# A linear attention fused with a routed MLP: the seam changed in three places, and the order inside one attention unit

## Chip, cores and metric

The kernel runs on one core of a Trainium2 chip. The metric is the device time of one execution in microseconds (us); smaller is better.

## What is computed

Two computations follow each other. The first is a linear attention with a decaying state (batch 4, 8 heads, 768 steps, head size 48); the second is a mixture of experts with 8 experts (3072 rows of 384, hidden size 1024), where each row goes through one expert, chosen by its logits, and is scaled by its gate. Cut to what matters:

```
for t in range(S):
    cur = einsum('bhd,bhe->bhde', u * k[t], v[t])
    y[t] = einsum('bhd,bhde->bhe', r[t], state + cur)
    state = w[t][..., None] * state + einsum('bhd,bhe->bhde', k[t], v[t])
x = y as rows of 384
logits = x @ w_gate + modality_bias[modality_id]
e_idx = argmax(logits, axis=1)
probs = exp(logits - max); probs /= probs.sum() + 1e-09
for e in range(E):
    mask = e_idx == e
    out[mask] = gate_w[mask] * (relu(x[mask] @ w1[e]) @ w2[e])
```

All data are float32.

## The kernel before

**Attention.** The 3072 rows are cut into 24 units of 128 steps. The loop `for i in range(-2, NU)` (NU = 24) calls `att_iter(i)`, which works on three units at once: it prepares unit a = i + 2, forms the products of unit m = i + 1 and finishes unit z = i. Preparing means two scans on VectorE (`B` backwards, L316, and `E` forwards, L322, with a reciprocal between them), then `K` (`mk_k`, L252) and `G = r * k` (L330) on GpSimd, and `R` (`mk_r`, L249) on VectorE, whose input ScalarE has copied to PSUM (`r_psum`). TensorE turns `K` (`turn`, L285), multiplies `K` with `R` (L371), uses `G` for the diagonal term (`delta`), updates the state `pU_st` and forms the output in `pY` (L410, L413). ScalarE scales the state and copies it to `SPb` (L260, L263). GpSimd computes `dV` (L326), and the row `xp` is `pY` plus `dV` (`x_rows`, L450 on VectorE, or L448 on GpSimd in some units).

**Routing.** `logits` (L467) multiplies finished rows with the gate's weights into the PSUM tile `pR_x`, which also holds the work areas of the routing and of the table below. The routing runs twice: for the first ten units and for the other fourteen (`CUT = (0, 10, 24)`). `route_a` finds the winning expert with five VectorE instructions (L500 to L506), `route_x` the gate's denominator: an exponential on ScalarE (L515), then three sums (L517) and an addition (L518) on GpSimd. `route_b` ranks the rows in each expert and gives each its place, `posT`. From then on `drain(1)` at the end of each unit sends one unit's finished rows to DRAM with an indirect DMA from GpSimd (`scatter`, L666), sorted by expert, into `xs`. Parts of the routing are hung into `att_iter` by a list `hooks`, from which each unit takes one entry.

**MoE.** It works on blocks of 512 rows (q = 0 to 5, the last with 416) and a half block. The expert of block 0 is known early, from the bias. Block 0's rows are loaded from `xs` by four DMAs, one per 128 rows (`rows_load`, L690, issued in unit i = NU - 3 behind the scatters). `blk_t(0)` transposes them on TensorE into three PSUM banks `pX`, `pK`, `pY` (L714: row block j = 0 to 3, in each of them three chunks of 128 features), and splits them into a rounded part `xh` (ScalarE, L722) and the rest `xo` (VectorE, L717), since float32 is computed with three fast products. `blk_up(q, f)` then computes piece f = 0 to 7 of the hidden layer: nine matmuls (L736), a relu on ScalarE (L745) and the rest of the split `h` on VectorE (L747). Two PSUM accumulators take turns in block 0. `w_split` splits the weights (L234, L235 and L240, L241).

**The table.** Which expert and which rows block 1 takes is computed by `table(0)`, a generator of small VectorE instructions on `pR_x` that is advanced with `next(tb)`. `loads()` finishes it, and then SyncE issues the loads of block 1, which read the table. `s` counts the pieces; `logits(NU - 1)`, the gate's logits of the last unit, are issued at s = 2.

**What sets the order.** Each engine carries out its instructions in the order in which this program issues them. A scheduler doesn't move them; a framework places the waits between engines.

## Time and profile before

| | |
|---|---|
| median of three runs | 337.26 us (335.92 to 337.66) |
| profiled execution, its own time | 336.07 us |
| its span, first to last instruction | 334.2 us |
| busy share of the span | TensorE 96%, VectorE 64%, ScalarE 61%, GpSimd 59% |
| mean granted clock of TensorE | 0.998 of full speed |

The profile is of one execution. Its span leaves out 1.9 us around the first and the last instruction. A share of busy time is a mean over the attention (up to about 118 us), the seam between it and the MoE, and the MoE, and the engines are used differently in each. In a row of the timeline the first number is the start, the second the time, then come engine, line of the kernel, operation, output and inputs; what stands in brackets at the end is how long the engine stood idle before it, and who released it. PE is TensorE, DVE is VectorE, ACT is ScalarE, POOL is GpSimd, SP is SyncE.

### The profile page before, as it was taken

The numbers are of one execution on the slowest core, as the hardware profiler recorded it, in microseconds if no ns is written. First come the engines' busy times: TensorE is split into PE (matmuls) and PEld (weight loads), VectorE is DVE, ScalarE is ACT, GpSimd is POOL, SyncE is SP. The second block draws the span as 40 slices with busy tenths as digits, with TensorE's granted clock in tenths as the row PEclk, the third lists the DMA queues.
The fourth block names the chain that finished last, engine by engine and source line by source line (L and its number), as shares of the span: only waits on it lengthen the run. The fifth ranks groups of instructions, "written<-read, shape, count | busy, mean of one in ns | idle before, by whom it ended". The sixth has DMA issues, their size and how long they took to land. (4 is left out here: it accounts for less than half of the span.)

```text
span 334.2 us, 10519 instructions
## 1 busy us (share of the span) xinstructions
PE 320.0 (96%) x4086; PEld 292.3 (87%) x4086; DVE 213.8 (64%) x381; ACT 202.4 (61%) x451; POOL 197.7 (59%) x227
## 2 busy tenths in 40 slices
PE   7889999899989999999999999999999999999993
PEld 3689899898989977899889988998899889999992
DVE  6999999899998646795435945925550564054230
ACT  3877877698679956642423667765755855732150
POOL 7998899789999785676461870256034604440041
PEclk9999999999999999999999999999999999999999
DMA  7966778868778632426346055027444863360010
GB/s 263 370 210 198 240 224 268 265 188 249 226 236 283 206 91 97 95 101 228 124 151 182 0 151 183 0 73 174 179 167 165 234 218 94 95 214 2 2 75 29
DMA packets 32755, 54.73 MB, mean 164 GB/s; under 512 B 17665, under 2 KB 22457, under 8 KB 32696
## 3 DMA queue, kind: packets, MB, share of 16 engines
q1 hardware_dynamic: 29592, 44.51, 43.4%
q0 software_dynamic: 3104, 9.47, 7.5%
q8 instruction: 34, 0.56, 0.7%
q14 instruction: 25, 0.20, 0.2%
HBM read 53.92 MB, written 12.67 MB: 199 GB/s over the span
## 5 line engine op out<-in xcount | busy, mean ns | idle before, releaser
L235 POOL TENSOR_TENSOR wl<-raw,wh 128x768 fp32r<-128x768 f32 x20 | 38.5, 1929 | 73.7 <-ACT wh L234 73.6
L234 ACT CAST wh<-raw 128x768 fp32r<-128x768 f32 x48 | 39.4, 830 | 39.2 <-PE pU_d L758 24.6
L747 DVE SCALAR_TENSOR_TENSOR h<-pS_u,h 128x512 fp32r<-128x512 f32 (+2 forms) x39 | 23.2, 608 | 38.1 <-ACT h L745 31.8
L778 POOL DMA_INDIRECT out<-ot,xg x24 | 25.7, 1069 | 29.4 <-ACT ot L787 23.5
L235 DVE TENSOR_TENSOR wl<-raw,wh 128x768 fp32r<-128x768 f32 x28 | 31.0, 1113 | 15.1 <-ACT wh L234 14.8
L736 PE MATMUL pS_u<-xh,wh 128*128 128x512 f32 (+1 forms) x102 | 39.6, 389 | 0.0
L736 PE MATMUL pS_u<-xo,wh 128*128 128x512 f32 (+1 forms) x102 | 39.3, 385 | 0.0
L736 PE MATMUL pS_u<-xh,wl 128*128 128x512 f32 (+1 forms) x102 | 39.2, 384 | 0.0
L745 ACT ACTIVATE h<-pS_u 128x512 fp32r<-128x512 f32 (+1 forms) x34 | 19.8, 586 | 27.1 <-PE pS_u L736 25.3
L758 PE MATMUL pX_d<-wh,h 128*128 128x384 f32 x96 | 32.3, 337 | 0.0
L758 PE MATMUL pY_d<-wh,h 128*128 128x384 f32 x96 | 32.2, 335 | 0.0
L758 PE MATMUL pK_d<-wh,h 128*128 128x384 f32 x96 | 32.1, 334 | 0.0
L666 POOL DMA_INDIRECT xs<-xp,posT x24 | 26.2, 1092 | 9.2 <-issue 7.1
L330 POOL TENSOR_TENSOR G<-in 128x512 f32<-128x512 f32 x24 | 30.6, 1276 | 0.0
L316 DVE TENSOR_TENSOR_SCAN B<-in,pX_d 128x516 f32<-128x516 f32 x24 | 29.3, 1221 | 1.8 <-DMA in<-rkw 1.8
L252 POOL TENSOR_TENSOR K<-in,B 128x512 f32<-128x512 f32 x24 | 28.4, 1184 | 2.5 <-DMA in<-rkw 1.2
L322 DVE TENSOR_TENSOR_SCAN E<-in,pX_d 128x516 f32<-128x516 f32 x24 | 29.4, 1223 | 0.4
L758 PE MATMUL pU_d<-wh,h 128*128 128x384 f32 x80 | 26.7, 334 | 0.0
L747 DVE SCALAR_TENSOR_TENSOR h<-pT_u,h 128x512 fp32r<-128x512 f32 (+2 forms) x17 | 9.6, 577 | 24.6 <-ACT h L745 24.5
L413 PE MATMUL pY<-v,A 128*64 128x48 f32 x368 | 25.1, 222 | 0.0
L413 PEld LDWEIGHTS pY<-v,A 128*64 128x64 f32 x368 | 23.7, 138 | 0.0
L371 PE MATMUL pS<-R,K 64*64 64x128 f32 (+1 forms) x768 | 22.1, 250 | 0.5 <-DVE R L249 0.4
(246 smaller groups left out, 890.7 us busy)
## 6 DMA issues: line engine op xcount, KB each, us to landing
raw<-w SPq DMA_DIRECT2D x24, 768.0 KB
in<-rkw SPq DMA_DIRECT2D x60, 192.6 KB
v<-vt SPq DMA_DIRECT2D x24, 288.0 KB
xl<-xs SPq DMA_DIRECT2D x24, 192.0 KB
wg<-wf SPq DMA_DIRECT2D x8, 576.0 KB
raw<-w SPq DMA_DIRECT2D x16, 192.0 KB
xs<-zt SPq DMA_DIRECT2D x12, 193.0 KB
in<-rkw SPq DMA_DIRECT2D x3, 512.0 KB
```

The costliest lines, as they stand in the source:

```text
L234: nc.scalar.copy(out=wh[k][:, sl], in_=raw[k][:, sl])
L235: (eng or (nc.vector, nc.gpsimd)[k]).tensor_tensor(out=wl[k][:, sl], in0=raw[k][:, sl], in1=wh[k][:, sl].bitcast(F32), op=ALU.subtract)
L252: nc.gpsimd.tensor_tensor(out=wt(a, "K", [P, 4, P]), in0=quarters(k), in1=quarters(T["B", a][:, 1:517])[:, :, 1:129], op=ALU.mult)
L316: nc.vector.tensor_tensor_scan(out=Bt[:, 516:0:-1], data0=w[:, 516:0:-1], data1=d1[:, 516:0:-1], initial=0.0, op0=ALU.mult, op1=ALU.max)
L322: mark["E", i] = nc.vector.tensor_tensor_scan(out=Et, data0=w[:, 0:516], data1=d1[:, 1:2].to_broadcast([P, 516]), initial=1.0, op0=ALU.mul ...
L330: mark["G", i] = nc.gpsimd.tensor_tensor(out=wt(a, "G", [P, 512]), in0=r, in1=k, op=ALU.mult)
L413: nc.tensor.matmul(out=yh[64:P, g, sw, hh], lhsT=A[:, hh, g, 1 + sw], rhs=vs[:, g, hh] if sw else v[:, h * D:(h + 1) * D], start=new and n ...
L666: rows_apart("xs", nc.gpsimd.indirect_dma_start(out=xs[:, :], out_offset=bass.IndirectOffsetOnAxis(ap=posT[:, n:n + 1], axis=0), in_=T["xp ...
L736: nc.tensor.matmul(out=pp, lhsT=wsrc[0][:, f, c * P:(c + 1) * P], rhs=xsrc[:, c], start=(n == 0), stop=(n == 3 * KC - 1))
L747: nc.vector.scalar_tensor_tensor(out=h2[:, o:o + c1 - c0], in0=pp[:, c0:c1], scalar=0.0, in1=hh[:, c0:c1].bitcast(F32), op0=ALU.max, op1=A ...
L758: nc.tensor.matmul(out=X["y", q][j], lhsT=hsrc[:, j * P:(j + 1) * P], rhs=wsrc[1][:, f], start=(f == 0 and n == 0), stop=(last and n == 2))
L778: ins = nc.gpsimd.indirect_dma_start(out=out[:, :], out_offset=bass.IndirectOffsetOnAxis(ap=xg[0:n, j, 1:2].bitcast(I32), axis=0), in_=ot[ ...
```

## The change

It has five edits.

1. In unit i = 12 (`CUT[1] + 2`, the thirteenth), `route_a(0)` is no longer called from `hooks` at the end of unit i = 11, but behind the unit's backward scan and its reciprocal.
2. `route_x(0)` moves from the start of unit i = 12 to its end, directly ahead of the first `drain(1)`.
3. The last `G` (i = NU - 3) is computed by VectorE behind `R`, and no longer by GpSimd.
4. `blk_t(0)` splits block 0's rows in two groups of columns, 384 and then 128 (`slice(0, 3 * P)` and `slice(3 * P, BT)`), in each of them first the three `xh`, then the three `xo`. The other blocks are as before.
5. `table(0)` yields at two more places. Its twelve instructions behind the first sums are spread over s = 0 and s = 1, and `loads()` moves from s = 0 to s = 2.

```diff
+    def mk_g(i, eng, r, k):
+        mark["G", i] = eng.tensor_tensor(out=wt(i + 2, "G", [P, 512]), in0=r, in1=k, op=ALU.mult)
...
             nc.vector.reciprocal(out=w[:, 0:516:129], in_=Bt[:, 1:517:129])
+        if i == CUT[1] + 2:
+            list(route_a(0))
...
             mk_k(a, k)
-            mark["G", i] = nc.gpsimd.tensor_tensor(out=wt(a, "G", [P, 512]), in0=r, in1=k, op=ALU.mult)
+            if i < NU - 3:
+                mk_g(i, nc.gpsimd, r, k)
...
             mark["R", i] = mk_r(a)
+            if i == NU - 3:
+                mk_g(i, nc.vector, r, k)
...
             vec.tensor_reduce(out=te, in_=cm, axis=AX.X, op=ALU.add)
+            if ph == 0:
+                yield
...
                 tt(out=cm, in0=bc(i8), in1=t[:, :, None].to_broadcast(sh), op=ALU.is_equal)
+                if ph == 0:
+                    yield
...
-        def rest(m):
-            nc.vector.tensor_tensor(out=xo[m], in0=xt[m], in1=xh[m].bitcast(F32), op=ALU.subtract)
-
-        for m in range(KC):
-            if q:
-                rows_turn(q, m, w // 32, xt[m])
-            nc.scalar.copy(out=xh[m], in_=xt[m])
+        def high(m, c=slice(0, w)):
+            nc.scalar.copy(out=xh[m][:, c], in_=xt[m][:, c])
+
+        def rest(m, c=slice(0, w)):
+            nc.vector.tensor_tensor(out=xo[m][:, c], in0=xt[m][:, c], in1=xh[m][:, c].bitcast(F32), op=ALU.subtract)
+
+        for c in (slice(0, 3 * P), slice(3 * P, BT)) if q == 0 else ():
+            for m in range(KC):
+                high(m, c)
+            for m in range(KC):
+                rest(m, c)
...
         if i == CUT[1] + 1:
-            ra, tb = route_a(0), table(0)
-            hooks.extend([lambda: list(ra), lambda: hook_b(0)])
-        if i == CUT[1] + 2:
-            route_x(0)
+            tb = table(0)
+            hooks.extend([lambda: None, lambda: hook_b(0)])
         if i >= NU - 2:
-            hooks.append(lambda: next(tb))
+            hooks.append(lambda i=i: next(tb) if i == NU - 2 else None)
...
+        if i == CUT[1] + 2:
+            route_x(0)
         drain(1)
...
             blk_up(q, f)
-            if s == 0:
+            if s < 2:
+                next(tb), next(tb)
+            if s == 2:
                 loads()
             if s == 2:
                 logits(NU - 1)
```

What this moves, engine by engine, is read from the two built programs. First GpSimd in unit i = 12, before (`ex` holds the exponentials, `xp` the rows with the gate's denominator as one more column):

```order
L510 COPY xp_392<-tidi 128x10
L517 TENSOR_TENSOR ex_1594<-ex_1594 128x10x4
L517 TENSOR_TENSOR ex_1594<-ex_1594 128x10x2
L517 TENSOR_TENSOR ex_1594<-ex_1594 128x10
L518 TENSOR_SCALAR xp_392<-ex_1594 128x10
L326 TENSOR_TENSOR dV_1606<-v_1373,dT_1537 128x384
L252 TENSOR_TENSOR K_1608<-in_91,B_1600 128x512
L330 TENSOR_TENSOR G_1610<-in_91 128x512
L666 DMA xs<-xp_392,posT 29184x386
```

and now:

```order
L518 COPY xp_392<-tidi 128x10
L331 TENSOR_TENSOR dV_1600<-v_1373,dT_1537 128x384
L252 TENSOR_TENSOR K_1602<-in_91,B_1586 128x512
L255 TENSOR_TENSOR G_1604<-in_91 128x512
L525 TENSOR_TENSOR ex_1712<-ex_1712 128x10x4
L525 TENSOR_TENSOR ex_1712<-ex_1712 128x10x2
L525 TENSOR_TENSOR ex_1712<-ex_1712 128x10
L526 TENSOR_SCALAR xp_392<-ex_1712 128x10
L678 DMA xs<-xp_392,posT 29184x386
```

The three sums and the addition have moved behind `dV`, `K` and `G`; they stand directly ahead of the first scatter, which waits for the addition.

Second, ScalarE at the seam, where it rounds block 0's rows, with the engine that each instruction waits for in brackets. Before:

```order
L461 COPY xT_2884<-pT_('x', 0)_2883 128x384 [waits PE_49]
L722 CAST xh_2890<-pX_x_0_2894 128x512 [waits PE_49]
L722 CAST xh_2890<-pK_x_1_2895 128x512 [waits PE_49]
L722 CAST xh_2890<-pY_x_2_2896 128x512 [waits PE_49]
L461 COPY xT_2917<-pT_('x', 1)_2916 128x384 [waits PE_49,Activation_49]
```

and now:

```order
L469 COPY xT_2884<-pT_('x', 0)_2883 128x384 [waits PE_49]
L729 CAST xh_2890<-pX_x_0_2894 128x384 [waits PE_49]
L729 CAST xh_2890<-pK_x_1_2895 128x384 [waits PE_49]
L729 CAST xh_2890<-pY_x_2_2896 128x384 [waits PE_49]
L729 CAST xh_2890<-pX_x_0_2894 128x128 [waits DVE_49]
L729 CAST xh_2890<-pK_x_1_2895 128x128 [waits DVE_49]
L729 CAST xh_2890<-pY_x_2_2896 128x128 [waits DVE_49]
L469 COPY xT_2923<-pT_('x', 1)_2922 128x384 [waits PE_49,Activation_49]
```

Three casts have become six. The first three wait for TensorE as the wide ones did (for its transposes of the fourth row block), the last three for VectorE's subtraction of 384 columns from the same bank.

Third, VectorE in the first pieces of block 0: the end of the table, with `h` of the pieces 0 and 1. Before:

```order
L575 TENSOR_TENSOR pR_x<-cs,pR_x 128x8
L576 TENSOR_TENSOR pR_x<-pR_x,hd_2832 128x8
L577 TENSOR_REDUCE t2(0, 1)_2930<-pR_x 128x1
L579 TENSOR_TENSOR t2(0, 1)_2930<-pR_x,t2(0, 1)_2930 128x1
L747 SCALAR_TENSOR_TENSOR h_0_2977<-pS_u_0_2967,h_0_2977 128x512
L582 SCALAR_TENSOR_TENSOR pR_x<-pR_x,t2(0, 1)_2930 128x1
L583 TENSOR_SCALAR tab<-pR_x 128x1
L585 TENSOR_SCALAR tabe<-pR_x 128x1
L586 TENSOR_SCALAR tab<-pR_x 128x1
L589 SCALAR_TENSOR_TENSOR tab<-pR_x,e0f 128x1
L606 TENSOR_TENSOR fA<-fA,hd_2832 128x8
L747 SCALAR_TENSOR_TENSOR h_1_3035<-pS_u_1_3025,h_1_3035 128x512
```

and now, where `h` of piece 0 follows the reciprocal that ends the split of the rows:

```order
L746 RECIPROCAL xg_2727<-xg_2727 128x4
L767 SCALAR_TENSOR_TENSOR h_0_2970<-pS_u_0_2960,h_0_2970 128x512
L615 TENSOR_SCALAR fs_2828<-pR_x 128x9
L616 SCALAR_TENSOR_TENSOR fA<-pR_x,fs_2828 128x8
L574 TENSOR_TENSOR pR_x<-pR_x,cs 128x8
L575 TENSOR_REDUCE pR_x<-pR_x 128x1
L579 TENSOR_TENSOR pR_x<-pR_x,fA 128x8
L580 TENSOR_REDUCE pR_x<-pR_x 128x1
L581 TENSOR_TENSOR pR_x<-cs,pR_x 128x1
L584 TENSOR_SCALAR pR_x<-pR_x 128x1
L585 TENSOR_TENSOR pR_x<-cs,pR_x 128x8
L767 SCALAR_TENSOR_TENSOR h_1_2995<-pS_u_1_2985,h_1_2995 128x512
```

The `h` of piece 0 now goes ahead of the table's twelve instructions, and the `h` of piece 1 ahead of the last three of them and of the five that end with the writing of `tab` (below the rows shown). The order on TensorE and SyncE is unchanged.

## Rows read from the trace of the kernel before

**Rows 1.** Busy time by stretch: us, PE, PEld, DVE, ACT, POOL busy (x instructions), clock, DMA share, GB/s

```profile
140.00:160.00 20.00, 20.00 (x112) 19.39 (x111) 13.78 (x41) 7.85 (x13) 13.53 (x19) 1.00 0.42 150
```

**Rows 2.** Timeline of POOL, the first two scatters and the last one

```profile
66.11 0.87 POOL L517 TENSOR_TENSOR ex<-ex 128x40 f32<-128x40 f32 x3 [1.93 <-ACT ex L515]
67.06 0.28 POOL L518 TENSOR_SCALAR xp<-ex 128x10 f32<-128x10 f32 x1
...
71.50 1.19 POOL L666 DMA_INDIRECT xs<-xp,posT  x1 [0.86 <-POOL G L330]
...
73.50 1.19 POOL L252 TENSOR_TENSOR K<-in,B 128x512 f32<-128x512 f32 x1
...
76.08 1.02 POOL L666 DMA_INDIRECT xs<-xp,posT  x1 [0.17 <-issue]
...
109.94 1.27 POOL L330 TENSOR_TENSOR G<-in 128x512 f32<-128x512 f32 x1
111.38 1.01 POOL L666 DMA_INDIRECT xs<-xp,posT  x1 [0.17 <-issue]
```

**Rows 3.** Waits of SP's queue: us in total, times, longest

```profile
SPq L690 <- DMA xs<-xp,posT: 2.4, 1, 2.4
```

**Rows 4.** Timeline of PE at the seam

```profile
119.53 0.38 PE L714 MATMUL pX_x<-cs,xl 128*128 128x128 f32 x1 [0.17 <-DMA xl<-xs]
...
120.00 0.38 PE L714 MATMUL pX_x<-cs,xl 128*128 128x128 f32 x1
...
121.08 0.38 PE L714 MATMUL pX_x<-cs,xl 128*128 128x128 f32 x1 [0.46 <-DMA xl<-xs]
...
122.86 0.50 PE L736 MATMUL pS_u<-xo,wh 128*128 128x512 f32 x1
```

**Rows 5.** Timeline of DVE, unit 13's routing and the end of the attention

```profile
64.33 0.24 DVE L500 TENSOR_REDUCE mx<-pR_x 128x10 f32<-128x80 f32 x1 [1.07 <-PE pR_x L467]
...
112.94 0.56 DVE L450 TENSOR_TENSOR xp<-pY,dV 128x384 f32<-128x384 f32 x1 [1.30 <-PE pK L285]
```

**Rows 6.** Timeline of ACT in unit 13

```profile
65.79 0.24 ACT L515 ACTIVATE ex<-pR_x 128x80 f32<-128x80 f32 x1 [0.64 <-DVE oh L506]
...
70.22 0.64 ACT L263 COPY SPb<-pU_st 64x192 f32<-64x192 f32 x2
```

**Rows 7.** Line of the scatter: POOL's queue events, ns min/median/max, first and last start

```profile
L666 POOLq EVENT_SEMAPHORE  x1: 2474/2474/2474, 68.1 to 68.1; - x1
```

**Rows 8.** Timeline of PE, the transposes of unit 15's K

```profile
75.16 0.27 PE L285 MATMUL pT<-cs,K 64*128 64x64 f32 x1
```

**Rows 9.** Timeline of DVE at the seam

```profile
118.32 0.56 DVE L450 TENSOR_TENSOR xp<-pU,dV 128x384 f32<-128x384 f32 x1 [1.04 <-PE pU L413]
122.11 0.69 DVE L717 TENSOR_TENSOR xo<-pX_x,xh 128x512 fp32r<-128x512 f32 x1 [3.23 <-ACT xh L722]
```

**Rows 10.** Timeline of ACT at the seam

```profile
119.05 0.48 ACT L461 COPY xT<-pT_('x', 0)_2883 128x384 f32<-128x384 f32 x1 [0.95 <-PE pT_('x', 0)_2883 L460]
121.49 0.59 ACT L722 CAST xh<-pX_x 128x512 fp32r<-128x512 f32 x1 [1.97 <-PE pX_x L714]
```

**Rows 11.** Timeline of DVE, the table and piece 0

```profile
124.00 0.14 DVE L603 TENSOR_SCALAR fs<-pR_x 128x9 f32<-128x9 f32 x1
...
126.30 0.68 DVE L747 SCALAR_TENSOR_TENSOR h<-pS_u,h 128x512 fp32r<-128x512 f32 x1
126.90 0.15 DVE L582 SCALAR_TENSOR_TENSOR pR_x<-pR_x,t2(0, 1)_2930 128x1 f32<-128x1 f32 x1
...
127.29 0.15 DVE L589 SCALAR_TENSOR_TENSOR tab<-pR_x,e0f 128x1 int32<-128x1 f32 x1
```

**Rows 12.** Timeline of DVE, the table's first part, in the bank of the logits

```profile
115.12 0.17 DVE L550 TENSOR_SCALAR pR_x<-pR_x 128x8 f32<-128x8 f32 x1 [0.59 <-PE pR_x L467]
```

**Rows 13.** Timeline of ACT, piece 0's relu

```profile
125.06 0.60 ACT L745 ACTIVATE h<-pS_u 128x512 fp32r<-128x512 f32 x1 [0.62 <-POOL wl L241]
```

**Rows 14.** Timeline of PE, the last unit's logits

```profile
129.30 0.52 PE L467 MATMUL pR_x<-cs,xT 128*64 128x8 f32 x12
```

More of the change, by code (lines that the diff above doesn't have):

```diff
@@ L714, in blk_t @@
                     nc.tensor.transpose(out=xt[m][:, j * P:(j + 1) * P], in_=xl[:, j, m], identity=ident)
-        def rest(m):
-            nc.vector.tensor_tensor(out=xo[m], in0=xt[m], in1=xh[m].bitcast(F32), op=ALU.subtract)
-        for m in range(KC):
-            if q:
-                rows_turn(q, m, w // 32, xt[m])
-            nc.scalar.copy(out=xh[m], in_=xt[m])
+        def high(m, c=slice(0, w)):
[7 more added lines that the diff above has]
+                rest(m, c)
+        for m in range(KC if q else 0):
+            rows_turn(q, m, w // 32, xt[m])
+            high(m)
             if m:
                 rest(m - 1)
-        rest(KC - 1)
+        if q:
+            rest(KC - 1)
         nc.vector.reciprocal(out=xg[:, :, 0:1], in_=xg[:, :, 0:1])
```

## Prediction

> **What bounds the kernel now.** I read the busy shares by stretch first. Between 140 and 160 us TensorE is busy for 20.00 of 20.00 us [rows 1]: in the MoE it sets the time, so whatever delays its start there is carried to the end. The timeline of GpSimd came next, because the change touches it most. Its scatters of finished rows run from 76.08 to 111.38, nine with eight equal periods, so 35.30 / 8 = 4.41 us each, with 0.17 us idle before one [rows 2]: a chain of its own that hands on any delay. The waits of SyncE show where the two chains meet: block 0's rows (`xl`) are loaded only when the last scatter has landed, and SyncE waits 2.4 us for that [rows 3]. At this seam TensorE stands still 0.17 us before the second rows' transposes at 119.53 and 0.46 before the last rows' at 121.08, and its second matmul of the block starts at 122.86 [rows 4]. So the start of the MoE hangs on: last scatter, landing, `xl`, transposes, `xh` by ScalarE, `xo` by VectorE.
>
> **The 13th unit's scan ahead of the routing.** VectorE waited 1.07 us before the first routing instruction, for TensorE's logits [rows 5]. The scan fills that wait: about 1.0 us of lead for VectorE. I count it as nothing, since VectorE already has lead at the end of the attention: it waits 1.30 us for TensorE at 112.94 [rows 5], and the seam waits for rows that GpSimd has scattered.
>
> **The gate's sums at the unit's end.** The exponential moves behind the two state copies on ScalarE, which end at 70.22 + 0.64 = 70.86; it takes 0.24 and so ends at about 71.12 [rows 6]. GpSimd followed it 0.08 later (66.03 to 66.11). The three sums take 0.87, the addition of the constant runs from 67.06 to 67.34, so 1.23 from the start of the sums [rows 2]: they end at 71.20 + 1.23 = 72.43. Only then can the first scatter go. Before, it followed the end of its wait for `posT` (68.1 + 2.474 = 70.57 [rows 7]) with a lead of 0.93, started at 71.50 and took 1.19 [rows 2]. How it follows an instruction of GpSimd itself, with the queue held up until just before, the trace doesn't show: at most that 0.93, at least the 0.17 of the later scatters. I take 0.93, since it is the same scatter behind a held queue: end at 72.43 + 0.93 + 1.19 = 74.55, where it was 72.69: **+1.86**. By 0.17 and a later scatter's 1.02 it is 73.62, **+0.93**. Who waits: `K` of unit 15 came 0.81 behind the scatter and took 1.19 [rows 2]; it ends at 74.55 + 2.00 = 76.55, and TensorE's transposes of it started at 75.16 [rows 8]. TensorE loses 1.39 there (0.46 by the low end).
>
> **The last G by VectorE.** It takes 1.27 us out of GpSimd's chain ahead of the last scatter [rows 2]. On VectorE it stands in front of the 1.30 wait [rows 5]; a product of this size took 0.69 there with one input in PSUM [rows 9], and even the 1.27 of GpSimd fits. No cost. The last scatter therefore moves by 1.86 - 1.27 = +0.59 (low end -0.34; -1.27 if GpSimd makes up the whole delay on the way). The rows at the seam move with it. TensorE comes there 1.39 late, of which the waits for `xl` that it had, 0.17 + 0.46 [rows 4], take up 0.63: at most +0.76. **Term 1: +0.59**, from -0.63 (the most that those two waits give back, if GpSimd makes up its delay) to +0.76.
>
> **Rows by columns.** The reading that the code suggests is that 384 columns are cast while the last 128 are still loading. In the built order it is not so: the wait of each 384-column cast is for TensorE's fourth transpose into that bank, as the wide cast's was, and the 128-column casts wait for VectorE. So everything starts from the same moment, 121.49. Before: cast 0.59 [rows 10], `xo` from 122.11 for 0.69 [rows 9], matmul at 122.86, 1.37 behind the start [rows 4]. Now: a cast of 384 takes about 0.48 as the copy of that size does [rows 10], and VectorE starts 0.03 later, at +0.51. It does three subtractions of 384 before the first of 128; one took 0.56 [rows 9], and VectorE starts the next some 0.08 before the end that the trace gives (126.30 + 0.68 against 126.90 [rows 11]): the 128 columns of the first chunk start at 0.51 + 3 x 0.48 = +1.95. They take an estimated 0.30 (0.56 less two steps of the 0.13 that separate 384 from 512). The second matmul starts 0.06 later at +2.31. **Term 2: 2.31 - 1.37 = +0.94**. High end +1.17 with 0.56 for the narrow one; low end -0.14, if the casts could start with the third row block's transposes, at 120.00 and not the fourth's at 121.08 [rows 4], 1.08 sooner: 121.49 - 1.08 + 1.95 + 0.30 + 0.06 = 122.72.
>
> What the trace has on this is one row: VectorE waited 0.59 for TensorE's logits at 115.12 before it touched other columns of the same bank [rows 12]. The Trainium skill, in "PSUM — Partial Sum Buffer", section "PSUM bank collisions raise a hardware error", says that accesses of different engines to one PSUM bank are to be ordered by bank and quadrant and not by address. By that rule term 2 is the +0.94, and by addresses alone it would be the -0.14; the row agrees with the rule.
>
> **The table between the pieces.** Twelve instructions ran from 124.00 until `h` of piece 0 started at 126.30 [rows 11], though ScalarE had its half at 125.06 + 0.60 = 125.66 [rows 13]. Now `h` starts at 125.69 (on the old clock of the seam), the next 0.60 later [rows 11], then nine of the twelve (9/12 of 2.30 = 1.73) to 128.02, `h` of piece 1 to 128.62, three to 129.20, five from 126.90 to 127.44 [rows 11], so 0.54, to 129.74. The logits of the last unit go on TensorE behind piece 2 and write the bank in which the table computes: they wait for that and start at about 129.79, where they started at 129.30 [rows 14]. **Term 3: +0.49** (low end -0.2: the logits don't wait, and `h` 0.6 earlier frees the accumulator that TensorE stood for before piece 2). SyncE's loads for block 1 follow the table and go out 129.74 - 127.44 = 2.3 later; their rows are first used when all eight pieces are done, so five more pieces cover that (2.3 at most if they don't).
>
> **The sum**: 0.59 + 0.94 + 0.49 = +2.0 us. The profiled execution took 336.07, so 338.1; the median of the runs is 337.26, and on that scale it is 339.2. What a measurement can tell from no change is 0.5%, 1.7 us: the forecast lies just above it.
>
> **The rivals.**
> *GpSimd is not held up* (the other side: not slower). The first scatter follows the gate's constant as the later ones follow their predecessors, by 0.17, or GpSimd makes up its delay before the last scatter. For it: 0.17 before every scatter shown later [rows 2]. Against: the 0.93 at this very scatter. Term 1 is then -0.34, or -0.63 at the most, and the sum +1.09 or +0.80: 338.1 to 338.4, no change. It decides when the first scatter ends before about 74.2, since 0.3 less in term 1 brings the sum under 1.7.
>
> *The columns run as the code reads*, so the change of the built order costs no time: term 2 is -0.14, the sum +0.94, 338.2. Against it stands the order of waits, and the row at 115.12.
>
> *The lead is lost more than once*: if the queue of GpSimd no longer runs ahead, the second scatter also starts 0.93 instead of 0.17 behind, +0.76 more, and a third again. Sum +2.8 to +3.5, 340.0 to 340.8. Against it: nothing after the first scatter holds the queue.
>
> **How the numbers follow.** The forecast gets 0.54; its own range is +1.6 to +2.4 (upwards by the high ends of terms 1 and 2, 0.76 + 1.17 + 0.49, and as far down), and with 1.7 in its lowest part I split it 0.40 slower, 0.14 same. GpSimd not held up: 0.20, same. Columns as read: 0.06, same. Lead lost more than once: 0.08, slower. What I haven't seen, 0.12: 0.09 faster (a stage that the lead of VectorE or the shorter last chain shortens), 0.03 same. Together 0.09 faster, 0.43 same, 0.48 slower. The time is the forecast's, 339.2; the range goes from 337.0, the first two rivals together (-0.63 - 0.14 + 0.49 = -0.3), to 340.3, past the forecast's 339.7 and into the last rival.
>
> **What would show it.** Right: the first scatter ends near 74.5 and its first sum starts near 71.2; the last scatter starts at about 112.0; TensorE waits more than 1 us before a transpose of `K` near 75 to 76; the second up-projection matmul comes 2.2 to 2.3 behind the first cast; the logits of the last unit wait for the table. Wrong: a last scatter at or before 111.4, a second matmul within 1.5 of the first cast, or logits without a wait, each of which removes its term; a time under 337.5 would mean that at least two of them are wrong.

## The result, and the profile after

The changed kernel took 338.41 us in the median of 22 runs (336.77 to 341.40); the kernel before took 335.27 us in 22 runs on the same chips (334.15 to 338.92). The ratio is 1.0083, with a 95% interval from 1.0062 to 1.0105: slower by 2.8 us (0.0083 x 335.27), with 2.1 to 3.5 as its bounds.

The profiled execution took 337.27 us, with a span of 335.5 (before: 336.07 and 334.2). It is one of the faster executions of the changed kernel, and the profiled execution of before was one of the slower ones, so the two traces differ by 1.2 to 1.3 us and not by 2.8. What each trace shows is therefore read as distances inside one trace, and the times come from the runs.

**Unit 13.** GpSimd's timeline of the changed kernel (start, us, instruction, and in brackets the idle time before it and its releaser):

```profile
70.20 0.86 POOL L525 TENSOR_TENSOR ex<-ex 128x40 f32<-128x40 f32 x3 [2.95 <-ACT ex L523]
71.15 0.28 POOL L526 TENSOR_SCALAR xp<-ex 128x10 f32<-128x10 f32 x1
72.28 1.18 POOL L678 DMA_INDIRECT xs<-xp,posT  x1 [0.85 <-DMA in<-rkw]
...
74.28 1.18 POOL L252 TENSOR_TENSOR K<-in,B 128x512 f32<-128x512 f32 x1
...
76.86 1.01 POOL L678 DMA_INDIRECT xs<-xp,posT  x1 [0.17 <-issue]
```

and ScalarE's:

```profile
69.23 0.64 ACT L266 COPY SPb<-pU_st 64x192 f32<-64x192 f32 x2
69.89 0.24 ACT L523 ACTIVATE ex<-pR_x 128x80 f32<-128x80 f32 x1
```

GpSimd stands idle for 2.95 us until the exponential comes, and the first scatter starts 0.85 us after the addition (71.43 to 72.28) and not 0.17: the long lead that it had before stays, as rows 2 showed it. From the end of the state copies (69.87) to the end of the first scatter (73.46) it is 3.59 us, where it was 72.69 - 70.86 = 1.83 [rows 2, 6]: +1.76. But the copies themselves are 0.99 earlier, so that on the clock of the kernel the scatter ends only 0.77 later. That they are earlier can't be put down to the scan: in the trace of before TensorE had stood still for 1.11 us at 63.89, ahead of the logits and for no partner that the trace names, and the changed kernel's trace has no stall of that size there.

TensorE then waits for `K` of unit 15:

```profile
75.52 0.27 PE L288 MATMUL pT<-cs,K 64*128 64x64 f32 x1 [1.74 <-POOL K L252]
```

and behind that wait its granted clock falls. Busy time by stretch (the third number from the end is the granted clock, 1.00 being 2.4 GHz and 0.50 being 1.2 GHz):

```profile
74.00:76.00 2.00, 0.48 (x14) 0.48 (x14) 1.97 (x5) 0.32 (x2) 2.00 (x3) 1.00 0.95 308
76.00:78.00 2.00, 2.00 (x56) 1.82 (x54) 1.01 (x1) 1.76 (x4) 1.81 (x3) 0.69 0.35 96
78.00:80.00 2.00, 2.00 (x38) 2.00 (x38) 1.71 (x3) 1.47 (x7) 2.00 (x3) 0.50 0.74 196
80.00:82.00 2.00, 2.00 (x33) 2.00 (x30) 1.16 (x2) 0.84 (x3) 1.84 (x2) 0.50 0.76 234
82.00:84.00 2.00, 2.00 (x42) 1.79 (x43) 1.09 (x2) 0.43 (x2) 1.97 (x3) 0.60 0.83 278
84.00:86.00 2.00, 2.00 (x76) 1.93 (x67) 2.00 (x4) 1.92 (x6) 1.83 (x3) 1.00 0.08 29
```

From 74 to 76 us TensorE was busy for 0.48 of the 2 us. Then it is busy without a break, but on half its clock for nearly 7 us: (0.31 + 0.50 + 0.50 + 0.40) x 2 / 0.50 = 6.8. In the kernel before the clock stood at 1.00 in all of these stretches.

**The last G.** On VectorE it took 0.96, and the last scatter starts 38.66 us behind the first (110.94 - 72.28), where it was 39.88: 1.22 earlier. Yet SyncE issues the first load of block 0's rows at 116.22, later than the 115.86 of before:

```profile
108.31 6.28 SPq L229 DMA_DIRECT2D raw<-w  x6
116.22 2.60 SPq L702 DMA_DIRECT2D xl<-xs  x4
```

and the wait for the scatter has shrunk from 2.4 us [rows 3] to 0.8:

```profile
SPq L702 <- DMA xs<-xp,posT: 0.8, 1, 0.8
```

The weight loads of this unit are spread by manual dependencies on its marks `E`, `R` and `G`. The last of them now stands behind the moved `G`, and SyncE's queue reaches the rows later (114.59 instead of 112.68). In this trace the weight load is not the last to come, though: the 0.8 us are still a wait for the scatter. The rows' load starts 5.28 behind the last scatter's start, where it was 115.86 - 111.38 = 4.48.

**The seam.** TensorE's timeline of the changed kernel, from the fourth transposes to the last unit's logits:

```profile
121.27 0.28 PE L726 MATMUL pX_x<-cs,xl 128*128 128x128 f32 x1
...
123.05 0.50 PE L756 MATMUL pS_u<-xh,wh 128*128 128x512 f32 x1 [0.50 <-ACT xh L729]
123.83 0.50 PE L756 MATMUL pS_u<-xo,wh 128*128 128x512 f32 x1 [0.28 <-DVE xo L732]
...
130.86 0.52 PE L475 MATMUL pR_x<-cs,xT 128*64 128x8 f32 x12 [0.85 <-DVE tab L601]
```

and ScalarE's casts:

```profile
121.58 0.48 ACT L729 CAST xh<-pX_x 128x384 fp32r<-128x384 f32 x1 [0.66 <-PE pX_x L726]
...
122.69 0.30 ACT L729 CAST xh<-pX_x 128x128 fp32r<-128x128 f32 x1
123.15 0.27 ACT L729 CAST xh<-pK_x 128x128 fp32r<-128x128 f32 x1 [0.15 <-DVE xo L732]
```

Three new waits of TensorE stand here: 0.50 and 0.28 for the narrow columns, 0.85 for the table. The second matmul comes 2.25 us behind the first cast (before 1.37 [rows 4, 10]), the logits 7.03 behind that (before 129.30 - 122.86 = 6.44 [rows 4, 14]).

### The profile page after: what moved, and what is told of

It reads as the page before. It is cut to its first block, busy times and chain, and to the rows that moved or that the text cites. A ratio compares the mean times of both kernels' runs of the same rounds, so it can differ in the third digit from the quotient of the medians.

```text
span 335.5 us, 10523 instructions
## 1 busy us (share of the span) xinstructions
PE 321.5 (96%) x4085; PEld 294.5 (88%) x4086; DVE 215.0 (64%) x385; ACT 202.4 (60%) x454; POOL 196.3 (59%) x226
## 5 line engine op out<-in xcount | busy, mean ns | idle before, releaser
L255 POOL TENSOR_TENSOR G<-in 128x512 f32<-128x512 f32 x23 | 29.3, 1276 | 0.0
L421 PE MATMUL pY<-v,A 128*64 128x48 f32 x368 | 25.9, 225 | 0.0
L421 PEld LDWEIGHTS pY<-v,A 128*64 128x64 f32 x368 | 24.5, 142 | 0.0
L379 DVE TENSOR_TENSOR A<-pS,m 128x768 f32<-128x768 f32 x24 | 22.4, 935 | 2.2 <-PE pT L294 1.3
```

Source lines behind the costliest of these rows:

```text
L255: mark["G", i] = eng.tensor_tensor(out=wt(i + 2, "G", [P, 512]), in0=r, in1=k, op=ALU.mult)
L421: nc.tensor.matmul(out=yh[64:P, g, sw, hh], lhsT=A[:, hh, g, 1 + sw], rhs=vs[:, g, hh] if sw else v[:, h * D:(h + 1) * D], start=new and n ...
```

## The experiments

The first four kernels do one part of the change alone; the others follow in the order in which they ran. What each was expected to show stands ahead of its result: A is my account, B and C are its rivals. Between executions the start of block 0 moves by some us, so three distances inside a trace are used beside the times: TensorE's wait for `K` of unit 15; the start of the second up-projection matmul behind block 0's first cast; and the starts of the first and the last down-projection of whole blocks behind that cast. The table holds them for all traces, one execution of each kernel. The ratios of the four single parts add up to 1.0138, 4.6 us, against 2.8 for the whole change; each is known to about 1 us either way, so the times alone can't divide the cost, and the distances have to.

| kernel | wait for `K` of unit 15 (us) | first cast at (us) | second matmul | first down-projection | last down-projection | ratio of times (95%) |
|---|---|---|---|---|---|---|
| before | none | 121.49 | +1.37 | +19.33 | +181.79 | |
| whole change | 1.74 | 121.58 | +2.25 | +20.80 | +183.26 | 1.0083 (1.0062 to 1.0105) |
| unit_only | 1.60 | 124.53 | +1.36 | +19.33 | +181.78 | 1.0050 (1.0014 to 1.0086) |
| last_g_only | none | 123.99 | +1.36 | +19.33 | +181.78 | 1.0015 (0.9983 to 1.0046) |
| columns_only | none | 125.54 | +2.25 | +19.93 | +182.39 | 1.0034 (0.9993 to 1.0074) |
| table_only | none | 120.65 | +1.36 | +19.92 | +182.37 | 1.0039 (1.0005 to 1.0074) |
| scan_only | none | 122.27 | +1.36 | +19.33 | +181.79 | 1.0006 (0.9969 to 1.0042) |
| sums_only | 1.74 | 125.12 | +1.36 | +19.33 | +181.79 | 1.0042 (1.0007 to 1.0077) |
| table_logits_later | none | 123.85 | +1.37 | +19.10 | +181.55 | 1.0029 (0.9990 to 1.0067) |
| scan_g_table | none | 122.27 | +1.36 | +19.04 | +181.50 | 1.0022 (0.9985 to 1.0058) |
| columns_own_bank | none | 121.36 | +2.26 | +19.89 | +182.35 | one run |
| sums_early | none | 121.60 | +2.26 | +22.28 | +184.73 | 1.0072 (1.0039 to 1.0105) |
| whole_again | 1.35 | 120.02 | +2.25 | +20.83 | +183.28 | 1.0150 (1.0103 to 1.0198) |
| parts_kept | none | 119.87 | +1.37 | +19.05 | +181.50 | 1.0007 (0.9980 to 1.0033) |

**unit_only**: edits 1 and 2.

```diff
             nc.vector.reciprocal(out=w[:, 0:516:129], in_=Bt[:, 1:517:129])
+        if i == CUT[1] + 2:
+            list(route_a(0))
...
-            ra, tb = route_a(0), table(0)
-            hooks.extend([lambda: list(ra), lambda: hook_b(0)])
-        if i == CUT[1] + 2:
-            route_x(0)
+            tb = table(0)
+            hooks.extend([lambda: None, lambda: hook_b(0)])
...
+        if i == CUT[1] + 2:
+            route_x(0)
         drain(1)
```

> Edits 1 and 2 alone (scan ahead of the routing, the gate's sums at the unit's end). Theory A (the sums hold up the first scatter, K of unit 15 comes late, TensorE stands still for it and its granted clock falls to the lower level for some 6 us): first scatter ends 0.7 to 1 us later than in the kernel before, TensorE waits 1.5 us or more for K near 75 us, the last scatter is 0.7 to 1 us later, block 0's first cast 0.6 to 1.2 us later, and the time +0.6 to +1.2 us. Rival B (VectorE's lead of 1 us is carried to the end): last scatter and first cast earlier, time 0 to -1 us.

Measured: +0.50%, 1.7 us (0.5 to 2.9). TensorE waits for `K` in this trace too:

```profile
76.90 0.27 PE L285 MATMUL pT<-cs,K 64*128 64x64 f32 x1 [1.60 <-POOL K L252]
...
108.74 0.59 PE L400 MATMUL pY<-SPb,R 128*64 128x96 f32 x4 [1.98 <-issue]
```

The wait is A's; the fall of the clock behind it is not in this execution (there is one later, with a granted clock of 0.59 in 108 to 110 us and 0.56 in 110 to 112, at the second row). That row is a stall for which the trace names no other engine; most kernels here have one or more of about this size, at places that change. With them A's times on the kernel's clock were missed: the first scatter ends 2.15 us later than before and the last starts 2.06 later (A: 0.7 to 1 each), the first cast is 3.04 later (A: 0.6 to 1.2). Of B nothing is left: the time is not shorter.

**last_g_only**: edit 3.

```diff
...
-            mark["G", i] = nc.gpsimd.tensor_tensor(out=wt(a, "G", [P, 512]), in0=r, in1=k, op=ALU.mult)
+            if i < NU - 3:
+                mk_g(i, nc.gpsimd, r, k)
...
             mark["R", i] = mk_r(a)
+            if i == NU - 3:
+                mk_g(i, nc.vector, r, k)
```

> Edit 3 alone (last G by VectorE). Theory A (the weight loads of that unit are issued on SyncE behind the moved G, which now ends some 2 us later, so that SyncE comes to block 0's rows later than the earlier scatter allows): last scatter 1.2 to 1.3 us earlier, the issue of the rows' first load within 0.4 us of the kernel before, first cast within 0.4, time -0.3 to +0.4 us. Rival B (the rows move with the scatter): first load and first cast 0.6 us or more earlier, time -0.6 us.

Measured: no difference that can be told from none (1.0015). The last scatter stands 38.58 behind the first, 1.30 earlier than before. SyncE's timeline:

```profile
107.79 7.96 SPq L229 DMA_DIRECT2D raw<-w  x6
116.61 1.93 SPq L696 DMA_DIRECT2D xl<-xs  x4
```

The rows' loads follow the last weight load (115.75) by 0.86, with no wait for the scatter left. Here SyncE, not the scatter, decides when the rows come: A. How much it is in us can't be read off, since this execution's attention was late as a whole: the rows' first load is 0.75 and the first cast 2.50 later than before, where A had both within 0.4.

**columns_only**: edit 4.

```diff
...
+        for c in (slice(0, 3 * P), slice(3 * P, BT)) if q == 0 else ():
+            for m in range(KC):
+                high(m, c)
+            for m in range(KC):
+                rest(m, c)
...
```

> Edit 4 alone (rows by columns). Theory A (nothing starts sooner, and VectorE reaches the first chunk's last columns behind three subtractions): the second up-projection matmul starts 2.2 to 2.3 us behind the first cast instead of 1.37, and the time is +0.9 us. Rival B (TensorE gets it back later, since some wait in block 0 shrinks by as much): same delay at the second matmul, time within 0.3 us of the kernel before.

Measured: +0.34% (-0.1 to +0.7), 1.1 us. TensorE's timeline has the two waits of the whole change:

```profile
127.01 0.49 PE L744 MATMUL pS_u<-xh,wh 128*128 128x512 f32 x1 [0.48 <-ACT xh L717]
127.79 0.50 PE L744 MATMUL pS_u<-xo,wh 128*128 128x512 f32 x1 [0.29 <-DVE xo L720]
```

The second matmul is late by 0.88, as A has it, but 0.28 of that comes back before the logits, which start 6.16 behind it and not 6.44: TensorE's stall before piece 2 has gone. 0.60 stays to the last down-projection. So A for the place, B for a third of the amount; the time alone fits both.

**table_only**: edit 5.

```diff
...
-            if s == 0:
+            if s < 2:
+                next(tb), next(tb)
+            if s == 2:
                 loads()
```

> Edit 5 alone (table between the pieces). Theory A (the last unit's logits wait for the end of the table): TensorE waits 0.8 us before these logits, they start 7.0 us behind the second up-projection matmul instead of 6.44, and the time is +0.5 us. Rival B (the earlier h of piece 0 pays for it): no wait or a wait that the shorter stall before piece 2 balances, time within 0.2 us. Rival C (the loads of block 1, which go out 2.3 us later, are not covered): VectorE waits for block 1's rows, time +1.5 us or more.

Measured: +0.39%, 1.3 us (0.2 to 2.5). The row that A named:

```profile
129.04 0.35 PE L467 MATMUL pR_x<-cs,xT 128*64 128x8 f32 x6 [0.85 <-DVE tab L593]
```

The logits start 7.03 behind the second matmul, and the last down-projection is late by 0.58. C is out: nothing more is lost in the blocks behind.

**scan_only**: edit 1. Its exponential, still at the unit's start, reads logits from which the row's maximum has not yet been taken, so in this kernel and in scan_g_table the gate's values are others; the instructions are the same.

```diff
             nc.vector.reciprocal(out=w[:, 0:516:129], in_=Bt[:, 1:517:129])
+        if i == CUT[1] + 2:
+            list(route_a(0))
...
-            ra, tb = route_a(0), table(0)
-            hooks.extend([lambda: list(ra), lambda: hook_b(0)])
+            tb = table(0)
+            hooks.extend([lambda: None, lambda: hook_b(0)])
```

> Edit 1 alone (the 13th unit's scan ahead of the routing; the gate's sums stay at the unit's start). Theory A (edit 2 is the harmful half of the pair, the scan costs nothing): no wait of TensorE above 1 us for K of unit 15, time -0.6 to +0.4 us. Rival B (the scan itself delays the routing, and with it the rank and the first scatter): first scatter and time as with both edits, +1 to +2 us.

Measured: 1.0006 (-1.0 to +1.4 us), and no wait for `K`: A, as far as these bounds tell. On TensorE the scan is not quite free: it waits 0.71 us for VectorE's `R` at 70.81, and 0.70 at the same place in scan_g_table.

**sums_only**: edit 2.

```diff
-        if i == CUT[1] + 2:
-            route_x(0)
...
+        if i == CUT[1] + 2:
+            route_x(0)
         drain(1)
```

> Edit 2 alone (the gate's sums at the unit's end; routing ahead of the scan as before). Theory A (the sums stand between G and the first scatter and hold it up): TensorE waits 1 us or more for K of unit 15, time +0.8 to +1.8 us. Rival B (only the two edits together do that): no such wait, time within 0.4 us.

Measured: +0.42%, 1.4 us (0.2 to 2.6), with TensorE's wait,

```profile
76.87 0.27 PE L285 MATMUL pT<-cs,K 64*128 64x64 f32 x1 [1.74 <-POOL K L252]
```

and, in the busy times by stretch, the clock at its lower level behind it:

```profile
78.00:80.00 2.00, 2.00 (x59) 1.93 (x50) 1.78 (x4) 1.91 (x7) 1.81 (x3) 0.70 0.58 177
80.00:82.00 2.00, 2.00 (x32) 2.00 (x32) 1.36 (x3) 1.72 (x6) 2.00 (x3) 0.50 0.71 180
82.00:84.00 2.00, 2.00 (x59) 1.88 (x60) 0.94 (x2) 0.44 (x2) 1.80 (x3) 0.94 0.98 314
```

All four traces with edit 2 have this wait (1.35 to 1.74), and none of the ten without it. A.

What the wait and the clock cost TensorE can be read from two distances inside a trace: from its first transposes of `K` of unit 13 to those of unit 15, which hold the wait, and from there to those of unit 18, three units on. The rows of the whole change:

```profile
64.88 0.27 PE L288 MATMUL pT<-cs,K 64*128 64x64 f32 x1
...
91.05 0.27 PE L288 MATMUL pT<-cs,K 64*128 64x64 f32 x1
```

of whole_again, the same kernel in another execution:

```profile
64.79 0.27 PE L288 MATMUL pT<-cs,K 64*128 64x64 f32 x1
...
75.45 0.27 PE L288 MATMUL pT<-cs,K 64*128 64x64 f32 x1 [1.35 <-POOL K L252]
...
88.66 0.28 PE L288 MATMUL pT<-cs,K 64*128 64x64 f32 x1 [0.52 <-POOL K L252]
```

and of table_logits_later, which has neither edit 1 nor edit 2:

```profile
67.47 0.27 PE L285 MATMUL pT<-cs,K 64*128 64x64 f32 x1
...
76.49 0.27 PE L285 MATMUL pT<-cs,K 64*128 64x64 f32 x1
...
89.72 0.27 PE L285 MATMUL pT<-cs,K 64*128 64x64 f32 x1
```

| kernels | unit 13 to 15 (us) | unit 15 to 18 (us) |
|---|---|---|
| neither edit: table_logits_later, last_g_only | 9.02, 9.02 | 13.23, 13.22 |
| edit 1, sums directly behind the routing: sums_early, parts_kept | 9.63, 9.65 | 13.21, 13.23 |
| edit 1, sums at the unit's start: scan_only, scan_g_table | 9.92, 9.92 | 13.31, 13.23 |
| edit 2, clock at 1.00 behind the wait: unit_only, whole_again | 10.65, 10.66 | 13.21, 13.21 |
| edit 2, clock falls: sums_only, whole change | 10.66, 10.64 | 14.13, 15.53 |

(The other traces have stalls without a partner in these stretches.) So edit 2 holds TensorE up by 1.6 us against neither edit, by 1.0 against edit 1 with the sums directly behind the routing, and the fall of the clock takes another 0.9 and 2.3 us. How much of that reaches the end of the kernel these distances don't tell.

**table_logits_later**: edit 5, with the logits behind piece 3.

```diff
...
-            if s == 2:
+            if s == 3:
                 logits(NU - 1)
```

> Edit 5, with the last unit's logits one piece later (behind piece 3). Theory A (the cost of the table between the pieces is the logits' wait for it and nothing else): no wait before the logits, and block 0's down-projection starts 19.05 to 19.2 us behind the first cast (19.33 in the kernel before, 19.92 with edit 5 alone), since the stall before piece 2 goes; time -0.3 to 0 us. Rival B (a wait of the same size appears behind piece 3 or at the second routing): down-projection 19.5 us or more behind the first cast.

Measured: first down-projection +19.10, 0.23 earlier than before and 0.82 earlier than with edit 5 alone. The logits' wait was the whole cost: A. In the time (1.0029, 0.9990 to 1.0067) a quarter of a us can't be seen.

**scan_g_table**: edits 1, 3 and 5, with the logits as above and this, against the changed kernel:

```diff
...
-        at = iter((("E", i), ("R", i), ("G", i)))
+        at = iter((("E", i), ("R", i), ("G" if i < NU - 3 else "R", i)))
```

> A version made from the parts: edit 1, edit 3 with the last weight load of that unit behind R instead of G, and edit 5 with the logits one piece later; no edit 2, no edit 4. Theory A (what costs is the sums at the end, the columns, the logits' wait and the load behind the moved G): last scatter 1.2 us earlier than its distance from the first in the kernel before, SyncE waits for it again before the rows, down-projection 19.05 to 19.2 us behind the first cast, time -0.3 to -1.2 us. Rival B (the attention is set by TensorE and its own gaps, so an earlier scatter is worth nothing): time -0.3 to +0.2 us.

Measured: 1.0022, no gain. The last scatter is 38.66 behind the first, and SyncE waits for it again:

```profile
SPq L702 <- DMA xs<-xp,posT: 3.5, 1, 3.5
```

The weight load was the reason for the vanished wait, as A says. But the rows' load comes 5.18 behind the last scatter's start, where it was 4.48 before. This distance lies between 3.4 and 5.3 in the traces here, so the 1.2 us of an earlier scatter are no more than what the landing varies by. For the time, B.

**columns_own_bank**: edit 4 with the fourth row block in a bank of its own.

```diff
...
+            x3 = pt("x3", "pU", (P, DM))
...
-                    nc.tensor.transpose(out=xt[m][:, j * P:(j + 1) * P], in_=xl[:, j, m], identity=ident)
+                    nc.tensor.transpose(out=xt[m][:, j * P:(j + 1) * P] if j < 3 else x3[:, m * P:(m + 1) * P], in_=xl[:, j, m], identity=ident)
...
```

> Edit 4 alone, with the fourth row block transposed into a PSUM bank of its own, so that the 384-column casts don't wait for it and the 128-column casts don't wait for VectorE. Theory A (besides the bank, VectorE's order costs: three subtractions go ahead of the first chunk's last columns): the first cast starts about one row block earlier, the second matmul still comes about 2.2 us behind it, and 1.6 to 2.3 us behind the fourth block's first transpose, against 1.78 in the kernel before and 2.65 with edit 4 alone (the lower end where the fourth rows land late). Rival B (the bank's waits are all of it): the second matmul 1.5 us or less behind the fourth block's first transpose.

TensorE's timeline of this kernel:

```profile
121.99 0.58 PE L715 MATMUL pU_x<-cs,xl 128*128 128x128 f32 x3 [0.43 <-DMA xl<-xs]
...
123.62 0.49 PE L745 MATMUL pS_u<-xo,wh 128*128 128x512 f32 x1
```

and VectorE's:

```profile
121.87 0.56 DVE L721 TENSOR_TENSOR xo<-pX_x,xh 128x384 fp32r<-128x384 f32 x1 [2.73 <-ACT xh L718]
122.35 0.55 DVE L721 TENSOR_TENSOR xo<-pK_x,xh 128x384 fp32r<-128x384 f32 x1
122.81 0.55 DVE L721 TENSOR_TENSOR xo<-pY_x,xh 128x384 fp32r<-128x384 f32 x1
123.28 0.68 DVE L721 TENSOR_TENSOR xo<-pU_x,xh 128x128 fp32r<-128x128 f32 x3
```

The first subtraction now starts before the fourth rows are there, and the narrow casts wait for nothing. The matmul comes 2.26 behind the first cast all the same, since VectorE works through 121.87 to 123.9 without a gap; it comes 1.63 behind the fourth transposes, 0.15 better than the 1.78 of before, with rows that landed late. A: the bank decides when the split begins, and VectorE's order decides how long it takes. Counted from the fourth transposes, the last down-projection starts at 121.36 + 182.35 - 121.99 = 181.72, and before at 121.49 + 181.79 - 121.08 = 182.20: with rows that land as late as these, columns in two banks were worth 0.48 us, in one execution.

**sums_early**: the whole change without edit 2, the sums directly behind the routing.

The edit is shown against the changed kernel:

```diff
         if i == CUT[1] + 2:
             list(route_a(0))
+            route_x(0)
...
-        if i == CUT[1] + 2:
-            route_x(0)
         drain(1)
```

> The whole change, but the gate's exponential and sums directly behind the routing at the unit's start (no edit 2). Theory A (edit 2 costs about 1 us in the attention, edits 4 and 5 cost 1.47 in the MoE): no wait of TensorE above 1 us for K of unit 15, last down-projection 183.2 to 183.3 us behind the first cast as with the whole change, time +1.2 to +2 us against the kernel before, 0.5 to 1.5 us less than the whole change. Rival B (the attention's part comes from something else): time as with the whole change, +2.5 us or more.

**whole_again**: the whole change, unaltered.

> The whole change again, beside the others. All theories: +2 to +3.5 us against the kernel before, last down-projection 183.26 us behind the first cast. Theory A: TensorE waits 1.5 us or more for K of unit 15 and its clock falls to the lower level after it. Rival B: no such wait in this execution, with a time of the same size.

Measured, on one chip: sums_early 1.0072 in 12 runs, whole_again 1.0150 in 6. Without edit 2 the wait for `K` is gone, as A has it, but the kernel is still slower than before by 2.4 us (1.3 to 3.5), where A gave 1.2 to 2 and B 2.5 or more: the time doesn't decide between them. Against whole_again it is 0.0078 x 334.6 = 2.6 us shorter by the ratios and 338.93 - 337.18 = 1.75 by the medians; the intervals touch at 1.0103 and 1.0105, so that about 0 to 5 us is what this pair allows. The whole change's 22 runs, measured apart, lie at 1.0083, only 0.4 us above it. sums_early missed A's distance: 184.73 and not 183.26. Its busy times by stretch say why:

```profile
121.00:123.00 2.00, 1.39 (x18) 1.13 (x18) 0.89 (x2) 1.40 (x4) 1.00 (x2) 1.00 0.00 0
123.00:125.00 2.00, 1.65 (x4) 1.14 (x5) 1.32 (x6) 1.65 (x8) 0.39 (x1) 0.65 0.00 0
125.00:127.00 2.00, 2.00 (x6) 1.53 (x5) 0.00 (x0) 0.29 (x2) 1.86 (x4) 0.50 0.00 0
127.00:129.00 2.00, 2.00 (x10) 1.64 (x9) 0.82 (x3) 1.32 (x2) 0.09 (x1) 0.99 0.00 0
```

In this execution the clock fell at the seam, behind the waits for the rows and for the narrow columns, and that cost 184.73 - 183.26 = 1.47 us more. whole_again's trace has the wait for `K` (1.35), but no fall of the clock, and it is the fastest of its six runs (335.34, the others 337.12 to 341.11). A, which gave 1.5 us or more and a fall, missed both; B, which had no wait, missed too. The last down-projection came at 183.28, as all had it.

**parts_kept**: edit 1 with the sums directly behind the routing, edit 3 with the weight load behind `R`, edit 5 with the logits one piece later. Against the changed kernel:

```diff
...
-        at = iter((("E", i), ("R", i), ("G", i)))
+        at = iter((("E", i), ("R", i), ("G" if i < NU - 3 else "R", i)))
...
-            if s == 2:
+            if s == 3:
                 logits(NU - 1)
```

> The parts that cost nothing by the runs so far: edit 1 with the gate's sums directly behind the routing, edit 3 with the last weight load of that unit behind R, edit 5 with the logits one piece later; no edits 2 and 4. Theory A: last down-projection 181.5 us behind the first cast (181.79 in the kernel before), time -0.5 to +0.2 us. Rival B (the lead of VectorE and the shorter chain of GpSimd are worth something at the seam): time -1 us or better.

Measured: 1.0007 (0.9980 to 1.0033), and in the MoE 0.29 us less than before. No version here beats the kernel before by what a run can show.

## Why the prediction was right

It forecast slower by 2.0 us, just above what a measurement tells from no change; measured were 2.8 (2.1 to 3.5). The predicted time of 339.2 us compares with 338.41, the range of 337.0 to 340.3 holds it, and "slower" was the likeliest case, with a chance of 0.48. The ratio is the sharper test, since the runs of before came out at 335.27 and not at 337.26. Half of the account is right by its mechanism, the MoE's 1.47 us of terms 2 and 3. For the attention's term 1 one of the prediction's own signs of being wrong came: a last scatter at or before 111.4, which it said would remove the term. It started at 110.94, and at 110.79 in whole_again. The time was lost all the same, but on TensorE and not on the path by the scatter and the rows that the term was summed along; that the sum came out near is to this extent luck. By its steps:

- **The scan as nothing**: right for the time, within -1.0 to +1.4 us (scan_only 1.0006). The wait of 1.07 that it was to fill stood behind a stall of TensorE of 1.11 us in the trace of before. That the state copies ended 0.99 us earlier in the whole change, so that the scatter's +1.86 became +0.77 on the kernel's clock, may come from that stall and is not shown to be the scan's lead. With edit 2, edit 1 adds nothing at `K` of unit 15 (10.65 with it, 10.66 without).
- **The gate's sums, +1.86 at the first scatter**: from the state copies on it was +1.76, with a long lead, 0.85, where I had taken 0.93 over 0.17. TensorE's loss was put at 1.39; the wait measured 1.35 to 1.74, and the delay 1.6 against kernels with neither edit. What the step left out is what comes of it. I let the waits for `xl` swallow most of TensorE's loss, and in the traces of the whole change and of sums_only the idle stretch is followed by some 6.8 and 3.4 us at the lower clock, which took 2.3 and 0.9 us more. The seam then waits for TensorE and not for the rows: in the whole change's trace the four groups of transposes follow each other without a wait. whole_again's trace, which lacks the fall, is 91.05 - 88.66 = 2.39 us ahead of it at `K` of unit 18, and 121.58 - 120.02 = 1.56 at the first cast: there the rows held TensorE up (0.33 before the fourth transposes), so part of the loss is given back at the seam, as the step had it, but less than it assumed.
- **The last G, no cost**: 1.22 of the 1.27 us were there at the last scatter. But I followed it on VectorE and GpSimd alone. On SyncE a weight load hung on its mark, which can hold the rows' load back by up to what the scatter gains; the step left this out. It decided in last_g_only; in the whole change's two traces SyncE still waited for the scatter (0.8 and 2.1 us). Its price in us stays open, since last_g_only shows no difference in time.
- **Term 1, +0.59**: probably too small, and by another path. What the runs give for edits 1 and 2 together is 1.7 (0.5 to 2.9), and 2.8 - 1.47 = 1.3 (0.6 to 2.0) is left for the attention in the whole change; 0.59 stands at the lower end of both.
- **Term 2, +0.94**: 0.88 at the second matmul, and of that 0.28 would come back if edit 5 didn't take the same stall away. (Its high end of 1.17 is 1.20 by its own parts, 0.94 + 0.56 - 0.30; nothing hangs on it.)
- **Term 3, +0.49**: 0.59, by the row of the wait that it named.
- **Terms 2 and 3** together: 1.43 forecast, 183.26 - 181.79 = 1.47 measured. The loads of block 1 were covered, as costed.
- **The rivals**: GpSimd was held up (0.85 before the first scatter). The lead was lost once only (0.17 before the second). The columns did not run as the code reads: the narrow casts waited 0.15 and more for VectorE.

The Trainium skill's rule in "PSUM — Partial Sum Buffer", section "PSUM bank collisions raise a hardware error", to order accesses of different engines by bank, agrees with those waits of 0.15 and with their absence in columns_own_bank, where the columns lie in two banks. From the first cast the split took 2.26 with two banks as well, by VectorE's order. But the prediction counted from the rows, and from the fourth transposes the second matmul came 2.65 behind with one bank (columns_only), 1.63 with two, and 1.78 before. So where the fourth rows land as late as in these traces (their transposes 1.05 behind the third's, 1.08 before), the 0.94 is the shared bank's, and the prediction's low end of -0.14 is what two banks gave: 1.63 - 1.78 = -0.15.

What stays open: how much of TensorE's loss behind edit 2 (1.6 us, and 0.9 or 2.3 more where the clock falls) reaches the end of the kernel. The times give 0.4 us (whole change against sums_early), 1.4 (sums_only) and 2.6 (whole_again against sums_early), with wide bounds. Open too is why the clock falls in two of the four traces with edit 2 and not in the others; each is one execution.

## What to carry to other kernels

Splitting the work ahead of a consumer into narrower pieces helps only if the consumer's first piece is ready sooner; where one engine must run all the wide pieces before the first narrow one, the first consumer waits for nearly all of it. And a piece that shares a PSUM bank with rows still to come starts only behind them, where the program orders its accesses by bank; with a bank of its own for the late rows it starts sooner (columns_own_bank). A step moved to another engine takes its marks with it: look through every queue, those of the DMAs too, for what hangs on the moved instruction. And a wait of TensorE of one to two us can cost more than its length (here 0.9 or 2.3 us more, or nothing), so a cost hidden "in slack" that makes TensorE stand still is to be counted with what its clock does next.

## What was not expected of the hardware

- After 1.74 us of waiting in two traces (whole change, sums_only) TensorE's granted clock fell to 0.50, for some 6.8 and 3.4 us; after waits of 1.60 (unit_only) and 1.35 (whole_again) it stayed at 1.00 there. The length of one wait doesn't tell which it will be: a stall of 1.13 at 83.02 (columns_own_bank) was followed by a fall, one of 2.06 at 60.21 (sums_early) was not. The Trainium skill describes this switch, by recent activity, between 1.2 and 2.4 GHz in "TensorE: Matmul & The Clock Gate", section "Part 1: The HAM clock gate (the "warmup" mystery)"; the traces agree on the two levels.
- TensorE has stalls without a partner in the trace, of up to 2.2 us, at places that change between kernels and executions (1.11 at 63.89 us before, 1.98 at 108.74 in unit_only), most often ahead of the logits near 60 us and of `pY` near 109. With them block 0's first cast moved between 119.87 and 125.54 us, while the distance from that cast to the last down-projection repeated within 0.05 us wherever the seam's code was the same and the clock didn't fall.
